# Loading two weight matrices by casting GpSimd transfers beside the loads of q, k and v, in a new order of instructions

## The chip, the cores and the metric

One core of one Trainium2 chip runs the whole program. The metric is device time in microseconds of one execution; medians over several executions are quoted. The record marks an execution as slow when it takes over 1.5% longer than the fastest of the same kernel; the others are called fast.

## The reference

A linear attention feeds a gated scan. Cut to what matters:

```python
q_s = softmax(q, axis=-1); k_s = softmax(k, axis=sequence)      # 8 batches, 8 heads, 576 x 64
kv  = einsum('bhsd,bhse->bhde', k_s, v)
x   = einsum('bhsd,bhde->bhse', q_s, kv)                        # as (8, 576, 512)
proj = x @ w_in                                                 # w_in 512 x 1024
val, gate = proj[..., :512], proj[..., 512:]
for t in range(576):
    h = exp(A_log) * h + val[:, t, :]                           # one state per batch and channel
    ys[:, t, :] = h
out = (gate * sigmoid(gate) * ys) @ w_out                       # w_out 512 x 512
```

Inputs are float32: 9.44 MB each of q, k and v, 2.10 MB of w_in, 1.05 MB of w_out, 2 KB of A_log. The output is 9.44 MB.

## The kernel before

The program is a list of tokens, `operation/engine.batch.part`, that fixes the order of instructions on every engine (A is ScalarE, D is VectorE, P is GpSimd). Each token calls a small function. Batches enter one by one: exp of q and its sums (`expq`, `qsum`), normalisation (`norm`), transposes on TensorE and their copies (`transp`, `tevac`), exp of k, cast of v (`vcast1`), the product kv and its normalisation (`kv`, `kvn`), the product with q (`xt` for batch 0) and its copies to bf16 (`xevac`). From there the work goes in 9 chunks of 512 positions: eight projections of 4 matmuls each (`val`, `gate`), scan, tanh, multiplications, output projection (`outp`), eviction (`oevac`), store.

All loads are issued by SyncE into one queue. The weights arrive as float32 in shared buffers and are cast by whichever engine the token names:

```python
def lwin(self, e, kt, h):                       # 8 of these, 256 KB each
    nc.sync.dma_start(out=buf("y", ("w", kt, h)),
                      in_=moe_w_in[kt * 128:kt * 128 + 128, h * Di:(h + 1) * Di])

def cwin(self, e, kt, h):
    copy(e, win[:, kt, h * Di:(h + 1) * Di], buf("y", ("w", kt, h)))

def lwout(self, e, j):                          # 2 of these, 512 KB each
    nc.sync.dma_start(out=buf("ob", ("w", j)),
                      in_=moe_w_out.rearrange("(j m p) c -> j p m c", j=2, p=128)[j])

def lalog(self, e):                             # the decay row
    nc.sync.dma_start(out=alog, in_=moe_A_log.rearrange("(o n) -> o n", o=1))

def _proj(self, dst, i, col):                   # called by val and gate
    ...
        for kt in range(4):
            nc.tensor.matmul(dst[:, a:z], lhsT=win[:, kt, col:col + 128],
                             rhs=xT[:, kt, s0:s0 + z - a], start=(kt == 0), stop=(kt == 3))
```

In the SyncE queue the order of bytes is q0, q1, k0 and v0, q2, w_in, k1, v1, q3, v2, k2, w_out, and so on (the digit is the batch).

The softmax here doesn't subtract the row's maximum and nothing guards it: scores larger than these inputs give would overflow.

## Time and profile before

| | before |
|---|---|
| median, range (3 executions, before the changed kernel was run) | 145.44 us, 144.34 to 145.5 |
| span of the profiled execution | 142.5 us |
| first projection starts | 22.9 us |
| last matmul ends | 138.5 us |
| HBM read, written | 31.46 MB, 9.44 MB |

The page opens with busy time, share of the span and number of instructions of each engine. A later part lists queues with packets, megabytes and share of the engines' time:

```profile
PE 119.6 (84%) x1269; PEld 61.7 (43%) x1284; DVE 114.6 (80%) x146; ACT 98.9 (69%) x138; POOL 92.2 (65%) x80
...
q1 hardware_dynamic: 24226, 42.08, 84.2%
```

TensorE is the busiest engine at 84%, which says little by itself, because the shares average a byte-bound start and a TensorE-bound rest. There is a single data queue. Of a table of stretches, the columns are length, then busy time with counts of PE, PEld, DVE, ACT and POOL, clock, DMA share, GB/s:

```profile
46.00:150.00 104.00, 91.82 (x898) 46.33 (x907) 81.63 (x102) 66.00 (x100) 59.22 (x44) 0.99 0.72 243
```

The second number is the work that TensorE still has in front of it at 46 us: 91.8 us. The last matmul starts its group at 137.42 and ends at 138.46, which is 92.5 us after the 46. So TensorE hardly idles in that stretch, and the end of the kernel is 46 us, plus what was left, plus a tail of 4.0 us to the end of the span. I call this number the work left at 46 us.

### The profile page before, as it was taken

What the parts mean: (1) busy time and instruction counts of PE and PEld (TensorE: products, weight loads), DVE (VectorE), ACT (ScalarE), POOL (GpSimd) and SP (SyncE); (2) the same over time, 40 slices, a digit from 0 to 9 for tenths busy, and PEclk for the clock granted to TensorE, in tenths of its full rate; (3) what the DMA queues carried; (4) which work ended last, traced back from release to release, by engine and by line L of the source; (5) the groups of instructions that cost most, each with busy time, mean ns of one, the idle gap of its engine ahead of it and who ended that gap; (6) DMA issues with size and microseconds to landing.
All of it is one profiled execution on the core that took longest, in us unless ns stands there. A gap on an engine that the chain in (4) does not pass through costs nothing.

```text
span 142.5 us, 3185 instructions
## 1 busy us (share of the span) xinstructions
PE 119.6 (84%) x1269; PEld 61.7 (43%) x1284; DVE 114.6 (80%) x146; ACT 98.9 (69%) x138; POOL 92.2 (65%) x80
## 2 busy tenths in 40 slices
PE   0024586987599999999999999999999999999980
...
DMA  4999999999999999999999999999543433007195
GB/s 111 401 399 391 391 390 389 391 393 391 389 389 392 391 391 391 387 404 403 394 325 382 399 240 208 263 408 392 110 83 121 181 147 147 0 0 289 71 343 190
DMA packets 24243, 42.29 MB, mean 297 GB/s; under 512 B 5666, under 2 KB 5922, under 8 KB 24227
## 3 DMA queue, kind: packets, MB, share of 16 engines
q1 hardware_dynamic: 24226, 42.08, 84.2%
...
HBM read 31.46 MB, written 9.44 MB: 287 GB/s over the span
## 4 chain that ended last, share of the span: by engine, by line
PE 70%; DMA 14%; DVE 5%; POOL 3%; issue 3%; SPq 2%; ACT 0%; POOLq 0%; ACTq 0%; DVEq 0%
PE pp L377 38%; PE po L423 21%; DMA kf<-in_k_dram 7%; DMA y<-in_moe_w_in_dram 6%; PE ax L290 4%; PE tp L271 3%; POOL eq L263 3%; SPq L188 2%; DVE qs L255 2%; PE pp L333 1%; PE ax L333 1%; DVE u L404 1%; DVE xT L194 1%; PE pp L423 1%; PE pp L360 1%
## 5 line engine op out<-in xcount | busy, mean ns | idle before, releaser
L377 PE MATMUL pp<-xT,win 128*128 128x512 bf16 (+1 forms) x308 | 68.0, 363 | 1.9 <-ACT xT L192 1.2
L408 POOL TENSOR_TENSOR z<-u,y 128x512 bf16<-128x512 f32 x29 | 37.3, 1297 | 24.2 <-DVE u L404 15.6
L377 PEld LDWEIGHTS <-win 128*128 128x128 bf16 x320 | 30.6, 99 | 31.5 <-issue 4.4
L396 DVE TENSOR_TENSOR_SCAN y<-decay,y,pp 128x512 f32<-128x512 f32 x32 | 39.6, 1262 | 1.4 <-PE pp L377 1.3
L263 POOL TENSOR_TENSOR eq<-eq,qs 128x1152 bf16<-128x1152 bf16 x16 | 33.8, 2119 | 7.9 <-DVE qs L258 7.7
L423 PE MATMUL po<-wout,z 128*128 128x512 bf16 x134 | 33.7, 379 | 0.3
L401 ACT ACTIVATE th<-pp 128x512 f32<-128x512 f32 x36 | 21.5, 597 | 15.8 <-PE pp L377 15.6
L404 DVE SCALAR_TENSOR_TENSOR u<-th,pp 128x512 f32<-128x512 f32 x36 | 24.4, 683 | 5.3 <-ACT th L401 4.8
L255 DVE TENSOR_REDUCE qs<-eq 128x36 f32<-128x2304 bf16 (+1 forms) x10 | 20.6, 2057 | 6.6 <-ACT eq L235 6.6
L271 PE MATMUL tp<-ident,eq 128*128 128x128 bf16 x108 | 10.9, 249 | 13.3 <-POOL eq L263 11.8
L235 ACT ACTIVATE eq<-qf 128x1152 bf16<-128x1152 f32 x16 | 18.3, 1158 | 5.3 <-DMA qf<-in_q_dram 5.3
L430 ACT ACTIVATE ob<-po 128x512 f32<-128x512 f32 x28 | 16.6, 599 | 7.6 <-PE po L423 7.6
L423 PEld LDWEIGHTS <-z 128*128 128x128 bf16 x148 | 13.9, 98 | 15.3 <-issue 1.0
L241 ACT ACTIVATE ek<-kf 128x2304 bf16<-128x2304 f32 (+1 forms) x10 | 17.2, 1736 | 0.5 <-DMA kf<-in_k_dram 0.5
L194 POOL CAST vb<-vf 128x1152 bf16<-128x1152 f32 (+1 forms) x14 | 14.9, 1080 | 3.7 <-DMA vf<-in_v_dram 3.6
L271 PEld LDWEIGHTS <-eq 128*128 128x128 bf16 x108 | 8.3, 111 | 17.4 <-POOL eq L263 13.2
L192 ACT ACTIVATE xT<-pp 128x504 bf16<-128x504 f32 (+1 forms) x20 | 7.8, 443 | 4.4 <-PE pp L333 2.6
L290 PE MATMUL ax<-vb,ek 64*64 64x65 bf16 x576 | 7.3, 199 | 1.5 <-ACT ek L241 1.1
L290 PEld LDWEIGHTS <-ek 64*64 64x64 bf16 x576 | 6.2, 112 | 4.7 <-issue 2.2
L192 ACT ACTIVATE eqT<-tp 128x768 bf16<-128x768 bf16 x8 | 6.5, 810 | 1.6 <-PE tp L271 1.6
L192 ACT ACTIVATE xT<-ax 128x1008 bf16<-128x1008 f32 x7 | 7.1, 1016 | 0.3 <-PE pp L360 0.3
L432 DVE TENSOR_SCALAR ob<-po 128x512 f32<-128x512 f32 x6 | 4.1, 684 | 3.2 <-PE po L423 3.2
...
## 6 DMA issues: line engine op xcount, KB each, us to landing
...
y<-in_moe_w_in_dram SPq DMA_DIRECT2D x8, 256.0 KB, 8.8
...
```

The lines of the kernel that those rows point to most:

```text
L192: nc.scalar.activation(out, in_, AF.Copy)
L235: nc.scalar.activation(buf("eq", b)[:, q2].rearrange("p c h d -> p h c d"), buf("qf", b)[:, 2 * q2:2 * q2 + 2].rearrange("p h (c d) -> p h ...
L255: nc.vector.tensor_reduce(s[:, 0, n].rearrange("p (a o) -> p a o", o=1), buf("eq", b)[:, h].rearrange("p q c h d -> p (q c h) d"), axis=AX ...
L263: eng[e].tensor_tensor(x, x, r.rearrange("p (a o) -> p a o", o=1) .broadcast_to([128, 2 * C, D]), ALU.mult)
L271: nc.tensor.transpose(tp[:, j, :], src[:, 6 * g + j, :], ident)
L290: nc.tensor.matmul(kvp[o:o + 64, h2, q2 * E1:(q2 + 1) * E1], lhsT=ek[r, 2 * q2 + hp2, c * D:(c + 1) * D], rhs=vb[r, 2 * q2 + hp2, c, :], s ...
L377: nc.tensor.matmul(dst[:, a:z], lhsT=win[:, kt, col:col + 128], rhs=xT[:, kt, s0:s0 + z - a], start=(kt == 0), stop=(kt == 3))
L396: nc.vector.tensor_tensor_scan(buf("y", (i, m)), a, buf("pp", ("v", i, m)), init, op0=ALU.mult, op1=ALU.add)
L401: nc.scalar.activation(buf("th", (i, m)), buf("pp", ("g", i, m)), AF.Tanh, scale=0.5)
L404: nc.vector.scalar_tensor_tensor(buf("u", (i, m)), buf("th", (i, m)), 1.0, buf("pp", ("g", i, m)), op0=ALU.add, op1=ALU.mult)
L408: eng[e].tensor_tensor(buf("z", i)[:, m], buf("u", (i, m)), buf("y", (i, m)), ALU.mult)
L423: nc.tensor.matmul(self._po(i, r, h), lhsT=buf("z", i)[:, m, r * 128:(r + 1) * 128], rhs=wout[:, m, self._cols(h)], start=(m == 0), stop=( ...
```

## The change

The intent is to take ten casts and ten loads out of the engines and the SyncE queue. A transfer issued by GpSimd can cast float32 to bf16 on its way, so the weights land ready to use and, being in another queue, need not wait behind q, k and v. The decay row goes to ScalarE's queue for the same reason. The list of tokens was rearranged as a whole; only its first lines are shown.

```diff
-lq.0.1 expq.0.1 lq.0.0 lq.1.- qsum.0.1 expq.0.0 norm/P.0.1 qsum.0.0 transp.0.2 expq.1.0 lk.0.0
-tevac/A.0.2 lv.0.1 norm/P.0.0 transp.0.0 lk.0.1 expk.0.0 expq.1.1 qsum.1.0 tevac/D.0.0
 ... (the rest of the old order is left out)
+lalog lq.0.0 lq.0.1 expq.0.0 lq.1.- lv.0.0 lk.0.0 lk.0.1 expq.0.1 expq.1.0 lv.0.1 qsum.0.0
+vcast1/A.0.1 expq.1.1 qsum.0.1 swin.1 swout lq.2.- norm/D.0.1 norm/P.0.0 qsum.1.0 expk.0.0
+transp.0.2 tevac/D.0.2 lv.1.- transp.0.0 vcast1/P.0.0 swin.0 tevac/D.0.0 transp.0.1 expk.0.1
 ... (the rest of the new order is left out)
+        def swin(self, e, h):
+            nc.gpsimd.dma_start(out=win[:, :, h * Di:(h + 1) * Di],
+                                in_=moe_w_in.rearrange("(k p) c -> p k c", p=128)[:, :, h * Di:(h + 1) * Di])
+
+        def swout(self, e):
+            nc.gpsimd.dma_start(out=wout, in_=moe_w_out.rearrange("(m p) c -> p m c", p=128))
 ...
         def lalog(self, e):
-            nc.sync.dma_start(out=alog, in_=moe_A_log.rearrange("(o n) -> o n", o=1))
+            nc.scalar.dma_start(out=alog, in_=moe_A_log.rearrange("(o n) -> o n", o=1))
```

`swin.1` is the gate half of w_in, `swout` all of w_out, `swin.0` the value half.

More of the change, by code (lines that the diff above doesn't have):

```diff
@@ L23 @@
 ORDER = """
-lq.0.1 expq.0.1 lq.0.0 lq.1.- qsum.0.1 expq.0.0 norm/P.0.1 qsum.0.0 transp.0.2 expq.1.0 lk.0.0
-tevac/A.0.2 lv.0.1 norm/P.0.0 transp.0.0 lk.0.1 expk.0.0 expq.1.1 qsum.1.0 tevac/D.0.0
-vcast1/P.0.2 lalog lv.0.0 expk.0.1 norm/P.1.0 vcast1/D.0.3 vcast1/P.0.0 qsum.1.1 vcast1/A.0.1
-transp.0.1 tevac/D.0.1 lq.2.- kv.0.1 lwin.0.0 lwin.2.0 lwin.3.0 kv.0.0 transp.1.0 tevac/A.1.0
-lwin.1.0 lwin.1.1 norm/P.1.1 kvn.0 lwin.0.1 xt.0.0.1 xt.0.1.1 cwin/P.2.0 expq.2.0 xevac/D.0.0.1
-transp.1.1 xt.0.0.0 tevac/D.1.1 xevac/A.0.1.1 transp.1.2 xt.0.1.0 xevac/D.0.0.0 lwin.2.1
@@ L30 @@
-cwin/D.0.0 cwin/P.1.0 cwin/P.3.0 lwin.3.1 cwin/P.1.1 xevac/D.0.1.0 expq.2.1 talog val.0.3 acol
-tevac/A.1.2 lk.1.- cwin/A.2.1 cwin/P.0.1 val.0.1 lv.1.- cwin/A.3.1 gate.0.0 decay/A.3 qsum.2.-
-scan.0.3 gate.0.3 tanh.0.0 scan.0.1 norm/P.2.0 decay/P.2 gmul.0.0 norm/P.2.1 tanh.0.3 vcast/P.1.1
-gmul.0.3 expk.1.1 transp.2.0 val.0.0 expk.1.0 lq.3.- scan.0.0 gate.0.2 val.0.2 tanh.0.2
-tevac/D.2.0 vcast/A.1.0 gate.0.1 zmul/P.0.3 transp.2.1 kv.1.1 gmul.0.2 scan.0.2 kv.1.0 lv.2.-
-tanh.0.1 lk.2.- lwout.0 kvn.1 lwout.1 gmul.0.1 lq.4.- xr.1 xrevac/D.1 xa.1.0 decay/A.0
@@ L36 @@
-tevac/D.2.1 expq.3.0 expq.3.1 lk.3.- xa.1.1 xbevac/A.1.1 zmul/P.0.0 xaevac/A.1.0 transp.2.2
-tevac/A.2.2 xbevac/D.1.0 gate.1.3 tanh.1.3 zmul/P.0.1 zmul/P.0.2 gate.1.2 qsum.3.- gmul.1.3
-val.1.0 vcast/P.2.0 tanh.1.2 gmul.1.2 vcast/P.2.1 val.1.3 expk.2.- norm/P.3.0 gate.1.1 scan.1.0
-transp.3.0 val.1.2 tanh.1.1 tevac/A.3.0 scan.1.3 norm/P.3.1 kv.2.0 cwout/A.0 gmul.1.1 scan.1.2
-gate.1.0 tanh.1.0 kv.2.1 expq.4.0 transp.3.1 cwout/P.1 kvn.2 expq.4.1 outp.0.2 tevac/D.3.1 xr.2
-decay/P.1 xa.2.0 transp.3.2 zmul/P.1.2 xrevac/D.2 gmul.1.0 outp.0.3 lv.3.- xa.2.1 qsum.4.-
@@ L42 @@
-val.1.1 lq.5.- zmul/P.1.0 zmul/P.1.3 oevac/A.0.2 xaevac/A.2.0 lv.4.- lk.5.- oevac/A.0.3
-vcast/P.3.1 xbevac/A.2.0 vcast/P.3.0 xbevac/A.2.1 scan.1.1 tevac/D.3.2 outp.0.0 outp.0.1 expk.3.-
-val.2.2 gate.2.1 scan.2.2 tanh.2.1 oevac/A.0.0 val.2.1 lk.4.- gmul.2.1 kv.3.1 kv.3.0 gate.2.0
-oevac/A.0.1 gate.2.2 expq.5.1 tanh.2.0 store.0.1 norm/P.4.0 zmul/P.1.1 scan.2.1 kvn.3 gmul.2.0
-tanh.2.2 val.2.3 transp.4.0 expq.5.0 norm/P.4.1 gmul.2.2 scan.2.3 outp.1.0 xa.3.0 xr.3 outp.1.1
-zmul/P.2.2 tevac/A.4.0 xrevac/A.3 lq.6.- qsum.5.- oevac/A.1.0 xa.3.1 xbevac/A.3.0 lv.5.-
@@ L48 @@
-xbevac/A.3.1 vcast/P.4.0 vcast/P.4.1 zmul/P.2.1 gate.2.3 outp.1.3 transp.4.1 tanh.2.3 val.2.0
-tevac/D.4.1 norm/P.5.1 gmul.2.3 scan.2.0 xaevac/A.3.0 zmul/P.2.3 transp.4.2 oevac/A.1.1 val.3.1
-val.3.3 expk.4.- scan.3.1 scan.3.3 tevac/D.4.2 norm/P.5.0 expk.5.- oevac/A.1.3 val.3.0 kv.4.1
-kv.4.0 gate.3.0 tanh.3.0 zmul/P.2.0 scan.3.0 outp.1.2 val.3.2 vcast/P.5.0 gate.3.2 gmul.3.0
-vcast/P.5.1 expq.6.0 oevac/A.1.2 tanh.3.2 expq.6.1 scan.3.2 kvn.4 transp.5.0 gate.3.1 outp.2.3
-gmul.3.2 tevac/D.5.0 xa.4.0 store.0.0 zmul/P.3.2 store.1.0 xr.4 zmul/P.3.0 tanh.3.1 xaevac/A.4.0
@@ L54 @@
-outp.2.0 gmul.3.1 xrevac/A.4 transp.5.1 oevac/A.2.3 kv.5.1 kv.5.0 store.1.1 lk.6.- xa.4.1
-gate.3.3 xbevac/A.4.1 qsum.6.- kvn.5 xbevac/A.4.0 outp.2.2 val.4.1 tanh.3.3 tevac/A.5.1
-oevac/A.2.0 gate.4.2 zmul/P.3.1 norm/P.6.0 gmul.3.3 tanh.4.2 transp.5.2 val.4.2 scan.4.1 gmul.4.2
-zmul/P.3.3 gate.4.0 tevac/A.5.2 gate.4.1 oevac/A.2.2 tanh.4.0 outp.3.1 scan.4.2 lv.6.- lq.7.-
-gmul.4.0 dtransp.6.0 vcast/P.6.0 xa.5.0 xa.5.1 tanh.4.1 gmul.4.1 store.2.1 oevac/D.3.1
-xbevac/D.5.1 norm/P.6.1 vcast/P.6.1 outp.2.1 expk.6.- val.4.0 xaevac/A.5.0 xbevac/D.5.0 outp.3.0
@@ L60 @@
-scan.4.0 kv.6.0 xr.5 zmul/P.4.2 dtransp.6.1 kv.6.1 val.4.3 xrevac/A.5 gate.5.1 zmul/D.4.1
-expq.7.1 gate.4.3 oevac/D.2.1 oevac/A.3.0 scan.4.3 zmul/P.4.0 tanh.5.1 tanh.4.3 kvn.6 expq.7.0
-outp.3.2 val.5.1 lv.7.- gmul.5.1 gmul.4.3 val.5.2 outp.3.3 scan.5.1 zmul/P.4.3 oevac/A.3.2 xa.6.1
-scan.5.2 zmul/P.5.1 outp.4.2 xbevac/A.6.0 store.2.0 store.3.0 qsum.7.- xbevac/A.6.1 xr.6
-vcast/P.7.0 oevac/A.3.3 xa.6.0 val.5.0 xrevac/A.6 outp.4.0 vcast/A.7.1 norm/P.7.1 val.5.3
-scan.5.0 oevac/A.4.2 xaevac/A.6.0 gate.5.3 scan.5.3 lk.7.- store.3.1 tanh.5.3 gate.5.2 tanh.5.2
@@ L66 @@
-outp.4.3 gmul.5.3 gate.6.0 gate.5.0 oevac/D.4.0 gmul.5.2 tanh.6.0 gmul.6.0 zmul/P.5.3 tanh.5.0
-val.6.2 gmul.5.0 val.6.3 outp.4.1 expk.7.- scan.6.2 gate.6.2 kv.7.1 kv.7.0 gate.6.3 oevac/A.4.1
-tanh.6.2 scan.6.3 dtransp.7.1 norm/P.7.0 gmul.6.2 kvn.7 zmul/D.5.2 val.6.1 dtransp.7.0 tanh.6.3
-oevac/A.4.3 zmul/P.5.0 val.6.0 gmul.6.3 outp.5.3 scan.6.1 scan.6.0 outp.5.2 zmul/D.6.2
-oevac/A.5.3 xr.7 xa.7.0 store.4.1 outp.5.1 xrevac/A.7 store.4.0 xa.7.1 xaevac/A.7.0 xbevac/D.7.0
-gate.6.1 xbevac/A.7.1 oevac/D.5.2 gate.7.0 val.7.0 zmul/P.6.0 tanh.6.1 tanh.7.0 gmul.6.1 gmul.7.0
@@ L72 @@
-outp.5.0 val.7.2 oevac/D.5.1 zmul/P.6.3 gate.7.2 scan.7.0 zmul/P.6.1 scan.7.2 outp.6.3 store.5.1
-val.7.3 oevac/A.5.0 gate.7.1 tanh.7.2 gmul.7.2 scan.7.3 tanh.7.1 gmul.7.1 gate.7.3 tanh.7.3
-val.8.2 val.7.1 gmul.7.3 zmul/P.7.0 val.8.0 outp.6.1 oevac/A.6.3 outp.6.0 scan.8.2 gate.8.1
-scan.7.1 scan.8.0 gate.8.2 zmul/D.7.3 oevac/A.6.1 tanh.8.1 gmul.8.1 gate.8.0 zmul/D.7.2
-zmul/D.7.1 oevac/A.6.0 tanh.8.2 outp.6.2 gmul.8.2 tanh.8.0 store.5.0 val.8.1 outp.7.2 val.8.3
-gmul.8.0 store.6.0 scan.8.1 oevac/A.6.2 oevac/A.7.2 zmul/P.8.2 gate.8.3 outp.7.3 tanh.8.3
@@ L78 @@
-scan.8.3 store.6.1 zmul/P.8.1 gmul.8.3 zmul/D.8.3 outp.7.1 oevac/A.7.3 outp.7.0 oevac/A.7.1
-zmul/P.8.0 store.7.1 oevac/A.7.0 outp.8.0 store.7.0 oevac/A.8.0 outp.8.1 store.8.0 outp.8.2
-outp.8.3.1 oevac/A.8.1 oevac/A.8.3.1 outp.8.3.0 store.8.1 oevac/D.8.2 store.8.3.1 store.8.2
-oevac/D.8.3.0 store.8.3.0
+lalog lq.0.0 lq.0.1 expq.0.0 lq.1.- lv.0.0 lk.0.0 lk.0.1 expq.0.1 expq.1.0 lv.0.1 qsum.0.0
+vcast1/A.0.1 expq.1.1 qsum.0.1 swin.1 swout lq.2.- norm/D.0.1 norm/P.0.0 qsum.1.0 expk.0.0
+transp.0.2 tevac/D.0.2 lv.1.- transp.0.0 vcast1/P.0.0 swin.0 tevac/D.0.0 transp.0.1 expk.0.1
@@ new lines @@
+lk.1.- qsum.1.1 kv.0.0 norm/P.1.0 tevac/D.0.1 vcast1/A.0.2 vcast1/P.0.3 norm/P.1.1 kv.0.1 kvn.0
+xt.0.1.0 xt.0.0.0 xevac/A.0.1.0 xevac/D.0.0.0 expq.2.1 xt.0.1.1 xevac/D.0.1.1 expq.2.0 transp.1.0
+lq.3.- tevac/D.1.0 xt.0.0.1 lv.2.- talog transp.1.1 xevac/D.0.0.1 gate.0.3 gate.0.0 qsum.2.- acol
+tevac/A.1.1 transp.1.2 tanh.0.3 tanh.0.0 tevac/A.1.2 gate.0.1 decay/P.2 lk.2.- vcast/P.1.1
+vcast/P.1.0 gmul.0.3 tanh.0.1 gmul.0.0 norm/P.2.0 val.0.3 gmul.0.1 decay/A.1 scan.0.3 val.0.0
+scan.0.0 decay/P.0 expk.1.0 expk.1.1 val.0.2 expq.3.1 gate.0.2 kv.1.0 kv.1.1 scan.0.2 kvn.1
@@ new lines @@
+norm/P.2.1 decay/P.3 tanh.0.2 transp.2.0 lq.4.- xr.1 xa.1.0 tevac/D.2.0 zmul/P.0.0 transp.2.1
+lv.3.- expq.3.0 lk.3.- gmul.0.2 lq.5.- zmul/P.0.3 xrevac/A.1 xa.1.1 xaevac/A.1.0 xbevac/A.1.1
+val.0.1 xbevac/A.1.0 gate.1.0 tevac/A.2.1 vcast/P.2.1 tanh.1.0 qsum.3.- scan.0.1 gmul.1.0 val.1.0
+transp.2.2 gate.1.2 expk.2.- vcast/P.2.0 zmul/D.0.1 zmul/P.0.2 gate.1.3 kv.2.0 tanh.1.2
+norm/P.3.0 tanh.1.3 scan.1.0 tevac/D.2.2 kv.2.1 gmul.1.3 expq.4.0 expq.4.1 gmul.1.2 norm/P.3.1
+outp.0.1 val.1.3 oevac/A.0.1 zmul/P.1.0 vcast/P.3.0 kvn.2 transp.3.0 lk.4.- gate.1.1 outp.0.3
@@ new lines @@
+tanh.1.1 tevac/A.3.0 scan.1.3 gmul.1.1 xa.2.0 xr.2 outp.0.2 zmul/P.1.3 xrevac/A.2 xaevac/A.2.0
+transp.3.1 oevac/A.0.3 xa.2.1 xbevac/A.2.0 vcast/P.3.1 val.1.2 qsum.4.- norm/P.4.0 outp.0.0
+xbevac/A.2.1 val.1.1 gate.2.2 expk.3.- tevac/D.3.1 scan.1.2 transp.3.2 lv.4.- val.2.2 tanh.2.2
+scan.1.1 oevac/A.0.0 zmul/P.1.2 zmul/P.1.1 expq.5.1 expq.5.0 oevac/A.0.2 tevac/D.3.2 gmul.2.2
+kv.3.1 kv.3.0 val.2.1 gate.2.1 scan.2.2 gate.2.0 vcast/P.4.0 lv.5.- scan.2.1 outp.1.0 tanh.2.1
+tanh.2.0 kvn.3 gmul.2.1 val.2.3 outp.1.1 gmul.2.0 expk.4.- xr.3 scan.2.3 xa.3.0 oevac/A.1.0
@@ new lines @@
+transp.4.0 gate.2.3 outp.1.3 xaevac/A.3.0 vcast/P.4.1 xrevac/A.3 xa.3.1 norm/P.4.1 oevac/A.1.1
+qsum.5.- kv.4.0 zmul/P.2.2 tanh.2.3 kv.4.1 gmul.2.3 kvn.4 xbevac/A.3.1 tevac/D.4.0 outp.1.2
+norm/P.5.0 xbevac/A.3.0 zmul/P.2.3 val.2.0 store.0.0 lk.5.- scan.2.0 zmul/P.2.1 val.3.1
+transp.4.1 tevac/D.4.1 gate.3.3 lq.6.- oevac/A.1.3 store.0.1 lk.6.- gate.3.1 oevac/A.1.2 xa.4.0
+transp.4.2 scan.3.1 expk.5.- tanh.3.3 val.3.2 gmul.3.3 vcast/P.5.0 val.3.0 tanh.3.1 tevac/A.4.2
+gmul.3.1 xaevac/A.4.0 zmul/P.2.0 scan.3.2 gate.3.0 scan.3.0 tanh.3.0 outp.2.0 kv.5.0 xr.4
@@ new lines @@
+transp.5.0 expq.6.1 gmul.3.0 norm/P.5.1 xrevac/D.4 lk.7.- store.1.1 expq.6.0 tevac/D.5.0 val.3.3
+vcast/P.5.1 kv.5.1 xa.4.1 transp.5.1 oevac/A.2.0 outp.2.1 scan.3.3 gate.3.2 tevac/A.5.1
+xbevac/A.4.0 xbevac/A.4.1 outp.2.3 transp.5.2 tanh.3.2 qsum.6.- gmul.3.2 val.4.3 expk.6.- val.4.1
+zmul/P.3.3 gate.4.1 lq.7.- oevac/A.2.1 store.1.0 zmul/P.3.1 scan.4.3 lv.6.- gate.4.0 tanh.4.1
+tanh.4.0 tevac/A.5.2 norm/P.6.0 scan.4.1 outp.2.2 val.4.0 store.2.0 zmul/P.3.2 kvn.5 gmul.4.1
+gmul.4.0 oevac/A.2.3 oevac/A.2.2 gate.4.2 zmul/P.3.0 tanh.4.2 norm/P.6.1 scan.4.0 gate.4.3
```

23 lines of the change are left out of this document (added).

## The prediction

> **What bounds the kernel now.** I read the strip of 40 slices first, to see which engine is full and when.
>
> ```profile
> PE   0024586987599999999999999999999999999980
> ...
> DMA  4999999999999999999999999999543433007195
> GB/s 111 401 399 391 391 390 389 391 393 391 389 389 392 391 391 391 387 404 403 394 325 382 399 240 208 263 408 392 110 83 121 181 147 147 0 0 289 71 343 190
> ```
>
> TensorE fills up only about slice 13 (46 us). The DMA engines are full from slice 2 on at about 390 GB/s. So the kernel has a start-up in which bytes are scarce, then a long stretch in which TensorE is scarce. A table of busy time by stretch puts numbers on it (columns: length, then PE, PEld, DVE, ACT, POOL busy with counts, clock, DMA share, GB/s):
>
> ```profile
> 22.90:29.30 6.40, 5.52 (x23) 2.29 (x24) 5.61 (x6) 4.67 (x8) 3.88 (x5) 1.00 1.06 392
> ...
> 34.80:38.00 3.20, 1.57 (x23) 0.86 (x24) 3.20 (x6) 3.20 (x5) 3.20 (x3) 1.00 1.06 393
> 38.00:46.00 8.00, 7.76 (x110) 3.84 (x111) 7.31 (x9) 6.78 (x9) 8.00 (x7) 1.00 1.05 389
> 46.00:138.50 92.50, 91.82 (x898) 46.33 (x907) 81.21 (x102) 66.00 (x100) 59.22 (x44) 1.00 0.78 264
> ```
>
> From 46 us TensorE idles 0.7 us in 92.5. No order of instructions can shorten that stretch except by having more done before it. The end of the kernel is therefore: the moment the first projection can start, plus a fixed amount of TensorE work, plus its idle time and slow clock in start-up, plus a tail. Now the start of the chain of waits (start, length, what):
>
> ```profile
> 3.52 10.61 DMA kf<-in_k_dram
> ...
> 14.53 9.10 DMA y<-in_moe_w_in_dram
> 23.68 0.61 POOL win L194
> 24.30 2.31 issue
> 26.75 2.13 POOL eq L263
> ```
>
> This names w_in as the last thing waited for until 24.3 us, which is the case for the change. But the timeline of the first 20 us shows the other branch, k and v of batch 0:
>
> ```profile
> 4.72 1.16 ACT L235 ACTIVATE eq<-qf 128x1152 bf16<-128x1152 f32 x1 [2.71 <-DMA qf<-in_q_dram]
> ...
> 9.65 1.16 ACT L235 ACTIVATE eq<-qf 128x1152 bf16<-128x1152 f32 x1 [2.30 <-DMA qf<-in_q_dram]
> ...
> 12.69 0.66 POOL L194 CAST vb<-vf 128x576 bf16<-128x576 f32 x1 [0.78 <-DMA vf<-in_v_dram]
> ...
> 15.79 0.66 POOL L194 CAST vb<-vf 128x576 bf16<-128x576 f32 x1 [0.36 <-DMA vf<-in_v_dram]
> ...
> 17.48 0.42 DVE L300 TENSOR_TENSOR kvc<-ax,kr 128x256 bf16<-128x256 f32 x1
> ```
>
> Each start behind a DMA marks a landing. They fit a straight line, landing = 3.1 us + megabytes queued so far / 0.39: q of batch 0 is 1.18 MB, predicted 6.1, and its second exp starts at 6.19; all of q0, q1, k0, v0 (4.72 MB) gives 15.2, seen 15.7; with q2 (1.18) and w_in (2.10) it gives 23.6, and the last w_in casts start at 23.7 and 24.3. After k and v come kv, its normalisation (17.48), four x products and their copies:
>
> ```profile
> 21.56 0.76 DVE L194 CAST xT<-ax 128x576 bf16<-128x576 f32 x1 [0.29 <-PE ax L312]
> ...
> 23.71 4.55 PE L377 MATMUL pp<-xT,win 128*128 128x512 bf16 x14 [0.22 <-POOL win L194]
> ```
>
> The last piece of x of batch 0 is ready at 22.3 us; the first projection starts at 22.9 and runs steadily from 23.7. So the branch through k0 and v0 and the branch through w_in end within about 1.4 us of each other. The tuner of the old order balanced them on a full DMA stream.
>
> **What the Trainium skill says.** "DMA: Bandwidth & Descriptors", section "SWDGE vs HWDGE vs iDMA": a cast inside a transfer can only be issued from GpSimd, whose software writes the descriptors. The trace before has no such transfer (its only data queue is SyncE's), so no number here. Same page, section "Issuing engines are not separate DMA queues": transfers from SyncE, ScalarE and GpSimd run on the same 16 DMA engines and interleave, so issuing from two saves only issue time. The trace agrees so far that the engines are the limit: share 1.05, 390 GB/s. Same page, section "Queues, rings and completion order": each DMA engine takes turns between queues by packets. That decides this case, and the trace before, with one data queue, cannot show it. "TensorE: Matmul & The Clock Gate", Part 1: TensorE runs at half rate until about 3.4 us of sustained work. The trace agrees: weight loads of the first projections are spaced 0.43 us (23.29, 23.72, 24.14 ... 26.28) and later 0.216 us (1.73 us for 8).
>
> **The change part by part.** Removed: 8 casts of w_in and 2 of w_out.
>
> ```profile
> L194 POOL CAST win<-y 128x512 bf16<-128x512 f32 x5 | 3.0, 612 | 2.8 <-DMA y<-in_moe_w_in_dram 2.7
> ...
> L192 ACT ACTIVATE win<-y 128x512 bf16<-128x512 f32 x2 | 1.3, 629 | 0.5 <-DMA y<-in_moe_w_in_dram 0.5
> ```
>
> GpSimd: 5 x 0.61 + 1.04 = 4.1 us; ScalarE: 2 x 0.63 + 1.05 = 2.3; VectorE: 0.42. None of it is on TensorE. On the path to the end lie only the waits it causes: TensorE waited 0.22 us for a cast and 0.66 us at 28.9 for a normalisation that GpSimd ran behind casts and a decay copy; between 34.8 and 38 us all three helpers are 100% busy and TensorE loses 1.6 of 3.2 us, part of it backlog, part the latency kv to x to projection, which stays. I book 0.9 + 0.6 = 1.5 us gain.
>
> Added: three GpSimd transfers (gate half of w_in, all of w_out, later the value half), 1.05 MB each as read. HBM bytes read stay at 31.46 MB, so at 0.39 MB/us nothing is saved if the read side paces them; only the order of bytes changes. The first two have no wait in front: GpSimd is free at 1.7 us (its last memset), so they can flow from about 5 us (estimate: the same 2.4 us from readiness to landing as q has, 0.74 to 3.1, plus a us to write descriptors). There they meet q0's second half, q1, k0, v0. By 5.2 us the SyncE queue has landed 0.82 MB of the 4.72 it needs for k0 and v0; 3.9 remain. With equal turns the 2.1 MB of weights are all through before those 3.9 MB end, and v0 lands at 3.1 + (4.72 + 2.10) / 0.39 = 20.6 us instead of 15.7. If GpSimd gets only a quarter of the turns, 3.9 / 0.29 = 13.4, so 18.6 us. If it cost nothing, 15.7. The value half comes third on GpSimd, after a cast of v0, and meets little of this. Early w_out buys nothing: the old kernel first uses it at 46 us.
>
> From v0 to the first projection the old kernel took 22.9 - 15.7 = 7.2 us; with w_in no longer in the way and a slightly tighter order of the x copies, I take 6.6. So the first projection: 27.2, 25.2 or 22.3 us, against 22.9: +4.3, +2.3, -0.6. I weigh them towards the middle: +2.3.
>
> Moved: the decay row to ScalarE's queue, before the table load at 0.73 us; its first exp waits for q until 4.72 anyway, so 0. One normalisation moves to VectorE, free then: 0. The order of everything else is new. In the long stretch TensorE cannot gain. The tail differs: the old one ends with half-row evictions (0.42 us) and 128 KB stores, the new one with two full ScalarE evictions (0.60) and a 256 KB store:
>
> ```profile
> out_dram<-ob SPq DMA_DIRECT2D x3, 256.0 KB, 2.9
> out_dram<-ob SPq DMA_DIRECT2D x2, 128.0 KB, 2.1
> ```
>
> (0.60 - 0.42) + (2.9 - 2.1) = 1.0 us at most; I take 0.7, as the old tail queued two small stores. Sum: +2.3 - 1.5 + 0.7 = +1.5 us; 145.4 + 1.5 = 146.9 us.
>
> **The rivals.** First, the weights are free: the second queue fills gaps and k0 and v0 are not late. For it: the chain names w_in, and both are off the old critical point. Against it: the DMA share is already full. Time: 145.4 - 0.6 - 1.5 + 0.7 = 144.0; if backlog falls further and the tail is equal, 142.5. Second, contention is full (equal turns or more): 145.4 + 4.3 - 1.5 + 0.7 = 148.9, and 150.5 if the late start also leaves batch 1 waiting: q, k, v of batches 0 and 1, q2 and all weights are 11.4 MB, so k1 lands at 32.3 us against 26.8. Third, GpSimd becomes the bound: writing descriptors might hold it longer than the 5 us of idleness it has before its first normalisation at 7.73. Beyond that each us delays the transposes, but those have slack until k0 and v0 land late, so it adds little: 147 to 149.
>
> **Range and chances.** 143.0 to 150.5 spans the rivals. Faster than 142.5 needs both free weights and a better order: 0.14. Slower than 148.3 needs nearly full contention: 0.33. Within 2%: 0.53.
>
> **What would show each step.** The v casts of batch 0 that wait for DMA: 15.8 moving to 18.5 to 21 proves contention; unchanged disproves it. The first projection at 25 us, and w_in no longer in the chain. Total GB/s in the first 20 us still about 390; well above would mean the cast paces differently, and a long landing time of the GpSimd transfers would mean a slow cast. TensorE still above 99% from 46 us; gaps there would mean the new order is at fault and the prediction wrong for a reason I did not weigh. The last store's landing shows the tail.

## The result, and the profile after

The changed kernel takes 149.61 us (median of 4, 148.91 to 149.74) against 145.38 us of the kernel before in the same rounds (144.34 to 145.5). The ratio is 1.0285, with a 95% interval of 1.0227 to 1.0343: slower. Ratios here and below are the mean time of one kernel's fast runs over that of the other's of the same rounds, so they are not quite the ratio of the medians. The spans of the two profiles, 142.5 and 147.7 us, differ by 5.2 us, more than the 4.2 us of the medians, because the profile of before fell on one of its quicker executions (144.23 us); the reason comes with experiment e10.

The strip of 40 slices of the changed kernel (3.7 us each), for TensorE and the bytes moved:

```profile
PE   0001415989699999999999999999999999999960
...
DMA  4999999999999999999999996952803300463374
GB/s 153 333 288 296 310 324 318 404 395 391 395 387 391 390 392 392 387 407 397 394 397 405 403 255 170 301 218 51 231 32 134 142 0 0 176 254 141 143 255 176
```

The DMA engines are as full as before from slice 2 on, but TensorE's ramp is later. In slices 3 to 7 the figure is 288 to 324 GB/s and not 390. The engines did not slow down: the view counts bytes written, and a casting transfer writes half of what it reads. The page's queues, and the issues of the weights with their size as written and the median time from issue to landing:

```profile
q1 hardware_dynamic: 22528, 38.93, 73.7%
q0 software_dynamic: 1584, 1.57, 6.4%
...
win<-in_moe_w_in_dram POOLq DMA_DIRECT2D x2, 512.0 KB, 11.1
...
wout<-in_moe_w_out_dram POOLq DMA_DIRECT2D x1, 512.0 KB, 16.6
```

The 1.57 MB in queue q0 are the 3.15 MB of weights after the cast. The trace also records single packets. Tabulated by queue (my own count in stretches of 1 us, not a view of the profile), it gives for the first 20 us:

```
stretch            packets per us            KB read per us
                   q0 (GpSimd)  q1 (SyncE)   q0          q1          sum
4 to 5 us          0            170          0           391         391
8 to 17 us         87 to 97     88 to 96     174 to 194  188 to 211  380 to 390
one packet, 8 to 17 us: q0 reads 2 KB, writes 1 KB, mean 96 ns; q1 moves 2304 B, mean 106 ns
```

(The counts include packets of 4 B; the means and KB of q0 leave them out. The trace gives what q0 writes; that it reads twice as much follows from the types, and fits the 31.46 MB read from HBM, as before.) The two queues take turns one for one, and the sum read stays about where it was. Now the timeline of the start (start, length, engine, line, what; in brackets the idle time and what ended it):

```profile
1.51 0.93 POOL L209 DMA_DIRECT2D win<-in_moe_w_in_dram  x1
2.44 0.75 POOL L213 DMA_DIRECT2D wout<-in_moe_w_out_dram  x1
...
14.66 0.66 POOL L192 CAST vb<-vf 128x576 bf16<-128x576 f32 x1 [5.21 <-DMA vf<-in_v_dram]
15.27 0.81 POOL L209 DMA_DIRECT2D win<-in_moe_w_in_dram  x1
...
22.20 0.67 POOL L192 CAST vb<-vf 128x576 bf16<-128x576 f32 x1 [3.98 <-DMA vf<-in_v_dram]
...
23.89 0.42 DVE L305 TENSOR_TENSOR kvc<-ax,kr 128x256 bf16<-128x256 f32 x1
...
27.71 0.58 PE L382 MATMUL pp<-xT,win 128*128 128x512 bf16 x1
```

The last casts of v0 follow their data at 22.2 us where the kernel before had 15.8, the normalisation of kv starts at 23.9 where it had 17.5, and the first projection at 27.7 where it had 22.9. The chain of waits (start, length, what) no longer contains w_in:

```profile
4.32 14.87 DMA vf<-in_v_dram
19.19 17.89 DMA qf<-in_q_dram
37.17 1.16 ACT eq L240
```

It now runs through v, and then through a load of q that lands at 37.1 us: until then the kernel waits for bytes of the SyncE queue. The same table of stretches as before:

```profile
46.00:150.00 104.00, 95.86 (x988) 48.45 (x998) 85.61 (x107) 68.76 (x102) 66.14 (x47) 0.99 0.69 243
```

The work left at 46 us is 95.9 us, 4.0 more than before. TensorE's last matmul ends at 142.89, 4.4 later. So the loss lies almost whole in the first 46 us, and the long stretch only passes it on.

### The profile page after: what moved, and what is told of

Read it like the earlier page. It is cut to its first block, busy times and chain, and to the rows that moved or that the text cites. A ratio compares the mean times of both kernels' runs of the same rounds, so it can differ in the third digit from the quotient of the medians.

```text
span 147.7 us, 3164 instructions
## 1 busy us (share of the span) xinstructions
PE 118.9 (81%) x1268; PEld 61.4 (42%) x1284; DVE 114.1 (77%) x142; ACT 96.0 (65%) x135; POOL 93.0 (63%) x80
## 3 DMA queue, kind: packets, MB, share of 16 engines
q0 software_dynamic: 1584, 1.57, 6.4%
HBM read 31.46 MB, written 9.44 MB: 277 GB/s over the span
## 4 chain that ended last, share of the span: by engine, by line
PE 63%; DMA 22%; DVE 6%; ACT 2%; SPq 2%; issue 1%; DVEq 0%; ACTq 0%
PE pp L382 36%; PE po L428 18%; DMA qf<-in_q_dram 12%; DMA vf<-in_v_dram 10%; PE ax L295 3%; PE tp L276 2%; SPq L186 2%; DVE y L401 2%; DVE qs L260 2%; DVE z L413 2%; ACT eq L240 2%; PE ax L338 1%; PE pp L338 1%; PE pp L428 1%; PE pp L365 1%
## 5 line engine op out<-in xcount | busy, mean ns | idle before, releaser
L413 POOL TENSOR_TENSOR z<-u,y 128x512 bf16<-128x512 f32 x31 | 39.4, 1286 | 22.8 <-DVE y L401 15.6
L268 POOL TENSOR_TENSOR eq<-eq,qs 128x1152 bf16<-128x1152 bf16 x15 | 32.1, 2148 | 6.4 <-DVE qs L263 6.4
L192 POOL CAST vb<-vf 128x1152 bf16<-128x1152 f32 (+1 forms) x15 | 16.0, 1085 | 11.6 <-DMA vf<-in_v_dram 11.6
L435 ACT ACTIVATE ob<-po 128x512 f32<-128x512 f32 x31 | 18.3, 597 | 7.0 <-PE po L428 7.0
L428 PEld LDWEIGHTS <-z 128*128 128x128 bf16 x148 | 13.8, 98 | 16.5 <-issue 1.0
L190 ACT ACTIVATE xT<-ax 128x1008 bf16<-128x1008 f32 (+1 forms) x8 | 7.7, 968 | 3.3 <-PE ax L317 2.0
L192 DVE COPY eqT<-tp 128x768 bf16<-128x768 bf16 x11 | 5.9, 532 | 0.9 <-PE tp L276 0.9
L190 ACT ACTIVATE eqT<-tp 128x768 bf16<-128x768 bf16 x7 | 5.7, 812 | 0.7 <-PE tp L276 0.7
```

The source lines that it names most:

```text
L190: nc.scalar.activation(out, in_, AF.Copy)
L192: eng[e].tensor_copy(out, in_)
L268: eng[e].tensor_tensor(x, x, r.rearrange("p (a o) -> p a o", o=1) .broadcast_to([128, 2 * C, D]), ALU.mult)
L413: eng[e].tensor_tensor(buf("z", i)[:, m], buf("u", (i, m)), buf("y", (i, m)), ALU.mult)
L428: nc.tensor.matmul(self._po(i, r, h), lhsT=buf("z", i)[:, m, r * 128:(r + 1) * 128], rhs=wout[:, m, self._cols(h)], start=(m == 0), stop=( ...
```

## The experiments

Theory 1: the GpSimd queue takes every second packet from the SyncE queue, k0 and v0 come late, and that is the loss. Rivals: the cast or the software queue itself is slow; GpSimd is held by its issues; the new order of instructions is at fault; or the bytes cost the same wherever they are put. The runs in one table, to which the text refers (a dash where it was not needed; e4's last five columns are from a profile in the slow state):

| run | median us | ratio | last cast of v0 | first projection | work left at 46 | last matmul ends | span |
|---|---|---|---|---|---|---|---|
| before | 145.4 | | 15.8 | 22.9 | 91.8 | 138.5 | 142.5 |
| changed | 149.6 | 1.0285 | 22.2 | 27.7 | 95.9 | 142.9 | 147.7 |
| e1 no weights | 142.2 | 0.982 | 15.9 | 21.4 | 88.7 | 134.8 | 139.6 |
| e2 w_out late | 148.4 | 1.0252 | 18.0 | 23.5 | 95.3 | 141.5 | 146.3 |
| e3 all late | 148.2 | 1.0213 | 15.6 | 23.5 | 95.3 | 141.6 | 146.3 |
| e4 old order, early | 149.8 fast | 1.0328 | 22.0 | 29.1 | 100.2 | 146.1 | 150.9 |
| e5 old order, late | 147.9 | 1.0175 | 16.8 | 24.3 | 94.9 | 140.9 | 145.8 |
| e6 hardware queue | 151.7 | 1.0461 | 22.6 | 28.1 | 97.8 | 145.7 | 149.9 |
| e7 k, v first | 151.8 | 1.0498 | 12.8 | 24.4 | 98.5 | 145.3 | 149.8 |
| e8 new order, SyncE | 152.5 | 1.0481 | 16.5 | 22.0 | 96.4 | 146.4 | 150.6 |
| e9 w_out on SyncE | 152.0 | 1.0464 | 16.4 | 24.4 | 96.1 | 144.9 | 149.6 |
| e10 row only | 145.1 | 0.9983 | 16.0 | 23.1 | 93.4 | 140.1 | 144.0 |
| e11 w_out only | 146.1 | 1.0048 | 16.0 | 23.0 | 92.5 | 139.1 | 143.4 |
| e12 as e8, mended | 148.1 | 1.0212 | 16.4 | 21.9 | 94.9 | 141.7 | 145.7 |

Medians of "before" were 144.67 beside e1 to e4, 145.56 beside e5 to e7, 145.8 beside e8 to e11 and 145.4 beside e12. e12 had 5 rounds, the others 3. The columns from the fourth on come from one execution of each run. The profiles of e2, e7 and e10 hold a stretch of 3.4 us at half clock before 46 us and those of e4, e8 and e9 one between 44 and 54 us, worth up to 1.7 us (see e10), so differences of that size between rows are not to be read as effects of an edit.

### e1_free: the new order without any load of weights

```diff
-... swin.1 swout ...          (three tokens taken out)
-... swin.0 ...
+    nc.vector.memset(win.rearrange("p k c -> p (k c)"), 0.01)
+    nc.gpsimd.memset(wout.rearrange("p k c -> p (k c)"), 0.01)
```

> The changed kernel with no weight transfers at all: w_in and w_out are filled with a constant by VectorE and GpSimd at the start, so the result is wrong on purpose; everything else, the new order included, is as in the changed kernel. Theory 1 (the weights take turns with q, k and v of batch 0 and push v0 back): v0 lands at about 15.7 us as in the kernel before, the first projection starts at 22 to 23 us instead of 27.7, and the time falls by about 5 us, to 143.5 to 145. Rival 2 (the new order of instructions is what costs): the time stays above 148. Rival 3 (the softer waits further on, on q of batch 3): the first projection is early, but the time falls by less than 3 us.

It took 142.18 us, ratio 0.982 (0.9738 to 0.9902); it fell more than expected. Its output is wrong, which doesn't matter for the time. From its timeline:

```profile
15.88 0.67 POOL L192 CAST vb<-vf 128x576 bf16<-128x576 f32 x1 [0.93 <-DMA vf<-in_v_dram]
...
21.39 3.09 PE L382 MATMUL pp<-xT,win 128*128 128x512 bf16 x8
```

v0 is on time again and the first projection starts 6.3 us earlier than in the changed kernel. The work left at 46 us falls by 95.86 - 88.65 = 7.2 us. The weights are 3.15 MB, at 0.39 MB/us 8.1 us of the DMA engines' time (an estimate from the rate of the strip). So in this order nearly all the time in which weights are read turns up as TensorE's work put off. What the new order costs by itself it does not tell: the old order was never run without weights, so the run cannot part the order from the bytes and casts that are gone.

### e2_wout_late: w_out moved out of the crowded start

```diff
-... qsum.0.1 swin.1 swout lq.2.- ...
+... qsum.0.1 swin.1 lq.2.- ...
-... vcast/P.1.0 gmul.0.3 ...
+... vcast/P.1.0 swout gmul.0.3 ...
```

> The changed kernel with only w_out's transfer moved, from the second place on GpSimd to behind the casts of v of batch 1 (about 30 us). Theory 1: 1.05 MB fewer compete before v0 lands, worth 1.05 / 0.39 = 2.7 us: v0 lands at about 19.5 us instead of 22.1, the first projection at about 25, the time about 147. If the amount of weights in flight did not matter (rival 2, the order), it stays at 149.6.

It took 148.44 us, ratio 1.0252 (1.0166 to 1.0338). The first projection came at 23.5 us, 4.2 earlier than in the changed kernel, and the median fell by about 1.2 us only, which the overlapping intervals of the two ratios do not tell from nothing. A miss. A table of stretches shows one place where the head start went (last three columns: granted clock, DMA share, GB/s):

```profile
36.00:38.00 2.00, 1.79 (x10) 0.73 (x8) 1.76 (x1) 2.00 (x6) 1.94 (x3) 0.51 1.12 290
38.00:40.00 2.00, 2.00 (x8) 0.75 (x7) 1.97 (x3) 1.05 (x2) 2.00 (x3) 0.64 1.10 322
```

After a pause TensorE ran at half clock for 3.4 us (36.0 to 39.5 us in the trace's clock records). And w_out, now read in front of k of batch 2, delayed that. The work left at 46 us is 95.3, only 0.6 below the changed kernel.

### e3_all_late: all three held until v0 has landed

```diff
-... qsum.0.1 swin.1 swout lq.2.- ...
+... qsum.0.1 lq.2.- ...
-... vcast1/P.0.0 swin.0 ...
+... vcast1/P.0.0 swin.1 swin.0 ...
-... vcast/P.1.0 gmul.0.3 ...
+... vcast/P.1.0 swout gmul.0.3 ...
```

> The changed kernel with both halves of w_in issued only after the first half of v of batch 0 has landed and been cast (about 11.5 us), and w_out behind the casts of v of batch 1. In the changed kernel a GpSimd transfer began to move about 4.7 us after its issue began, so these move from about 16 us, when v0 is in. Theory 1: v0 lands at about 15.7, the gate half of w_in at about 21.5, the first projection at 22 to 23, the time 144 to 145.5: no better than the kernel before by more than 1 us. Rival 2 (the new order): above 148. Rival 3 (GpSimd's issue or the cast itself is slow): between, as the weights are then late instead, first projection after 25 us.

It took 148.23 us, ratio 1.0213 (1.0145 to 1.0281). A miss again, and the one that changed my theory. (The transfers moved from 16.0 us as planned, 4.3 us after the issue began at 11.7; the 4.7 us of the expectation was a misreading of the trace.) From its timeline:

```profile
15.60 0.67 POOL L190 CAST vb<-vf 128x576 bf16<-128x576 f32 x1
...
23.46 3.59 PE L380 MATMUL pp<-xT,win 128*128 128x512 bf16 x8 [2.22 <-DMA win<-in_moe_w_in_dram]
...
42.38 2.12 ACT L244 ACTIVATE ek<-kf 128x2304 bf16<-128x2304 f32 x1 [2.18 <-DMA kf<-in_k_dram]
...
44.55 0.81 PE L293 MATMUL ax<-vb,ek 64*64 64x65 bf16 x72 [1.76 <-ACT ek L244]
```

v0 is as early as without weights. But w_in, issued at 11.7 us, lands only at 23.4, so TensorE waits 2.2 us for it, and w_out on its way holds up k of batch 2, for which ScalarE waits 2.2 us and TensorE behind it 1.8 us. The contention was moved, not removed. v0 alone does not set the end.

### e4_old_order_early: the old order with the three transfers as early as in the change

```diff
-  all tokens lwin, cwin, lwout, cwout
+  swin.0 swout before norm/P.0.1;  swin.1 after vcast1/P.0.2
```

> The kernel before, with its own order, but w_in and w_out loaded by the three GpSimd transfers as early as in the changed kernel (first half and w_out at the start, second half behind the first cast of v of batch 0), its SyncE weight loads and casts taken out. Theory 1: v0 again lands 5 to 6 us late (20.5 to 22 us), the first projection at 27 to 28, the time 148 to 150, as slow as the changed kernel although the order is the old one. Rival 2 (the new order is at fault): 143 to 145.5, the casts being saved.

Its fast runs took 149.54 and 150.14 us, ratio 1.0328 (1.0223 to 1.0433); two more were slow, and the profile is of one of these. As expected: without the new order, the early transfers alone lose as much as the whole change, and v0 is as late. From the timeline of the slow run, which I use for the landing only, not for times:

```profile
21.95 0.66 POOL L190 CAST vb<-vf 128x576 bf16<-128x576 f32 x1
...
29.05 1.46 PE L380 MATMUL pp<-xT,win 128*128 128x512 bf16 x3
```

### e5_old_order_late: the old order with the transfers held back

```diff
-  all tokens lwin, cwin, lwout, cwout
+  swin.0 after norm/P.0.1;  swin.1 after norm/P.0.0;  swout after decay/P.2
```

> The kernel before with its own order, weights by three GpSimd transfers as in the change, but issued so that they move only when k and v of batch 0 are nearly in: first half of w_in behind GpSimd's first normalisation (about 10 us), second behind its second (about 12.5 us), w_out behind a decay copy near 29 us. Theory 1: v0 lands at 15.7 to 16.5 us, the first projection at about 23, the time 143.5 to 145.5: the cast inside the transfer is worth 0 to 2 us once the competition is gone. If the cast or the software queue is itself slow (rival 3), the weights come after 27 us and the time is above 147.

147.93 us, ratio 1.0175 (1.0081 to 1.0269). A miss: I expected it to equal the kernel before. v0 came at 16.8, a microsecond late, the first projection at 24.3, and 94.9 us of work were left at 46 us, 3.1 more than before. Ten casts fewer on the engines did not pay for that. The first projection was 1.4 us late; what added the rest was not followed up.

### e6_hw_queue: plain float32 loads on ScalarE's queue at the same early places, cast by GpSimd

```diff
-            nc.gpsimd.dma_start(out=win[:, :, h * Di:(h + 1) * Di], ...
+            nc.scalar.dma_start(out=buf("y", ("w", kt, h)), ...        # and w_out likewise
+  cwin/P and cwout/P tokens after norm/P.1.0, before decay/P.2, after decay/P.3
```

> The changed kernel with the same weight bytes at the same early times, but uncast, from ScalarE's hardware queue into float32 buffers, and the casts to bf16 back on GpSimd where it is idle. Theory 1 (any second queue takes turns): v0 lands as late as in the changed kernel, 20 to 22 us, and the time is 148.5 to 151. Rival 3 (it is the cast, or GpSimd's software queue, that slows the shared engines): v0 lands before 18 us and the time is below 147.

151.67 us, ratio 1.0461 (1.0393 to 1.053). From its timeline:

```profile
22.63 0.67 POOL L192 CAST vb<-vf 128x576 bf16<-128x576 f32 x1 [0.65 <-DMA vf<-in_v_dram]
...
28.14 2.93 PE L382 MATMUL pp<-xT,win 128*128 128x512 bf16 x8
```

A hardware queue without a cast delays v0 to the same moment, 22.6 against 22.2 us. Its packets, too, alternate with those of SyncE's queue (from 8 to 16 us, 94 to 99 per us against 90 to 103, by the same count), and by 22.1 us it had read 2.56 MB of weights where the casting transfers had read 2.58. So neither the cast nor the software queue is needed for this delay; of the two kinds of second queue that were tried, both cause it. The time came 0.7 us above the expected range; GpSimd casts ten pieces in this run, and what they cost was not separated.

### e7_kv_first: k0 and v0 in front of q1

```diff
-lalog lq.0.0 lq.0.1 expq.0.0 lq.1.- lv.0.0 lk.0.0 lk.0.1 ... lv.0.1
+lalog lq.0.0 lq.0.1 expq.0.0 lv.0.0 lk.0.0 lk.0.1 ... lv.0.1 lq.1.-
 (softmax of q1 and transposes moved behind the x copies; weights as in e3)
```

> A try at a version that beats both: the changed kernel with k and v of batch 0 loaded before q of batch 1, w_in issued behind the first cast of v of batch 0 (about 10 us), w_out behind the casts of v of batch 1, and the work on q of batch 1 put behind the x copies of batch 0. Theory 1: the bytes in front of v0 are 3.54 MB, so v0 lands at 3.1 + 3.54 / 0.39 = 12.2 us; the gate half of w_in at about 20; the first projection at about 20, 2.5 us before the kernel before; the time 142 to 144, unless batch 1 (its q is later) leaves TensorE short between 25 and 45 us, then 144 to 146. If the landing of v0 does not set the end, the time stays with that of the run that only holds the weights back.

151.78 us, ratio 1.0498 (1.0405 to 1.0591), a clear miss. v0 was cast by 12.8 us, yet:

```profile
23.10 0.82 PE L274 MATMUL tp<-ident,eq 128*128 128x128 bf16 x6 [4.70 <-POOL eq L266]
...
24.37 2.93 PE L380 MATMUL pp<-xT,win 128*128 128x512 bf16 x8
```

TensorE sat 4.7 us in front of transposes of q1 that I had placed ahead of the first projection, and batch 1 came short later: 98.5 us left at 46 us. It tells that in this order an early v0 did not help while q1 was late, not what a well tuned order of this kind would give.

### e8_new_order_fifo: the new order with the old loading in the SyncE queue

```diff
-  swin.1 swout swin.0
+  lwin x8 after lq.2;  lwout x2 after lk.2;  casts on GpSimd and ScalarE
+  cwout/A.0 before expq.4.0;  cwout/P.1 after norm/P.3.1
```

> The changed kernel's order of instructions with the loading of the kernel before: w_in plain from SyncE's one queue behind q of batch 2, w_out behind k of batch 2, casts back on GpSimd and ScalarE. Theory 1, in the form it has after seven runs (the place of the weight bytes among the other bytes decides, first for v0, then for k of batch 2): v0 lands at 15.7 us, the first projection at 22 to 24, nothing waits for k of batch 2, and the time is 145.5 to 147, the new order keeping about 1.5 us of its own at the end (a wait for the last z, and a longer last store). Rival 2 (the order costs more than that): 148 or above.

152.5 us, ratio 1.0481 (1.0401 to 1.056). I had placed the casts of w_out badly, as the timeline of TensorE shows:

```profile
45.20 0.38 PE L428 MATMUL po<-wout,z 128*128 128x512 bf16 x1 [0.90 <-ACT wout L190]
...
48.98 0.59 PE L428 MATMUL po<-wout,z 128*128 128x512 bf16 x2 [3.40 <-POOL wout L192]
```

4.3 us of waits are mine and not the order's, so the run decides nothing about the order, and its time missed the expected 145.5 to 147. It does show the first projection at 22.0 us, 0.9 earlier than before.

### e9_wout_fifo: e3 with w_out as a plain load behind k of batch 2

```diff
-  swout after vcast/P.1.0
+  lwout x2 after lk.2;  cwout/A.0 before expq.4.0;  cwout/P.1 after norm/P.3.1
```

> The run in which the weights were held back, with only w_out taken from GpSimd and put plain on SyncE's queue behind k of batch 2, its two casts back on ScalarE and GpSimd. In the held-back run TensorE waited 1.8 us at 44.5 us for the exp of k of batch 2, which waited 2.2 us for its transfer. Theory 1: w_out's 1.05 MB no longer stand in front of it, k of batch 2 lands about 2 us earlier, and the time falls by 1.5 to 2 us, to about 146.3. If that wait was not what cost (a helper engine would have been next anyway), the time changes by less than 0.7 us.

151.99 us, ratio 1.0464 (1.0382 to 1.0547). The same misplaced casts cost 2.76 and 1.11 us, so its time, well above the expected 146.3, is inconclusive. ScalarE's wait for k of batch 2 fell from 2.18 to 0.36 us, which confirms what e3 said about w_out.

### e10_row_only: the kernel before with only the decay row on ScalarE

```diff
-            nc.sync.dma_start(out=alog, ...
+            nc.scalar.dma_start(out=alog, ...
-  lalog after vcast1/P.0.2
+  lalog first of all
```

> The kernel before with one part of the change alone: the decay row issued by ScalarE at the start instead of SyncE. All theories: no change, within 0.5 us of the kernel before; ScalarE's first exp waits for q until 4.7 us in any case, and SyncE's queue is full of waiting bytes.

145.11 us against 145.8, ratio 0.9983 (0.9893 to 1.0074): no change. Its runs fall in two groups, 144.2 to 144.4 and 145.9, as those of the kernel before do (144.1 to 144.4 and 145.3 to 145.9, with some others). The profile fell in the slower group, that of the kernel before in the quicker, and the two show a difference (weight loads, then a stretch, with the columns of above):

```profile
38.40 0.10 PEld L375 LDWEIGHTS <-win 128*128 128x128 bf16 x1 [1.72 <-issue]
38.78 0.15 PEld L375 LDWEIGHTS <-win 128*128 128x128 bf16 x1 [0.28 <-issue]
...
38.40:41.70 3.30, 3.08 (x7) 1.13 (x8) 2.22 (x3) 1.24 (x2) 3.30 (x4) 0.50 1.06 390
```

After the thin stretch between 34 and 38 us TensorE ran at half clock, from 38.27 to 41.68 us in the trace's clock records. In the profile of before, where TensorE resumed at 38.0 and not 38.4, the clock stayed at 1.00. Half of 3.41 us is 1.7 us lost; the work left at 46 us is 93.4 against 91.8 and the span 144.0 against 142.5.

The other executions bear this out. In the 32 executions of the kernel before that ran beside the experiments, the mean granted clock is 0.995 to 1.000 up to 144.9 us (one exception, 0.988), 0.986 to 0.988 from 145.4 to 146.3 us, and 0.976 in the three of 146.8 us that are marked slow. One stretch of 3.41 us at half clock in 144 us makes 0.988, two make 0.976. All four executions of the changed kernel have 0.993 or more, so between executions without such a stretch its loss is nearer to the 5.2 us of the spans than to the 4.2 us of the medians.

Why one execution has it and another has not stays open, but the clock records give a hint. In e2, e4, e7, e8, e9 and e10 the stretch lasts 3.41 us each time and begins a whole number of 3.41 us after the clock first became full: 28.03 + 3 x 3.41 = 38.27 in e10, 25.80 + 3 x 3.41 = 36.04 in e2. That first moment differs from profile to profile (26.47 in before). So it may be where this grid falls on the thin stretch, and not the 0.4 us by which TensorE resumed later, that decides; no run isolates it.

### e11_wout_soft: the kernel before with only w_out by a casting transfer

```diff
-  lwout.0 lwout.1 cwout/A.0 cwout/P.1
+  swout after zmul/P.0.3
```

> A try at keeping the good of both: the kernel before, with only w_out loaded by a casting GpSimd transfer, issued behind the first z product (about 34.5 us), so that it moves from about 39 us, when k of batch 2 is nearly in. This saves 1.04 us of GpSimd and 1.05 us of ScalarE near 44 us, where GpSimd is full. Theory 1: equal bytes at nearly the old place, so 0 to 1 us faster than the kernel before, 144 to 145.4. If w_out lands after 45.5 us (half the turns from 39 us: 1.05 / 0.2 = 5.3, so 44.4), TensorE waits for it and the time is 1 us above the kernel before.

146.08 us, ratio 1.0048 (0.997 to 1.0127): the same. At this place the transfer does no harm that can be seen, although the DMA engines are full there (share 1.12 from 39 to 44 us), and the two casts that it saves are worth nothing that can be seen.

### e12_new_order_fifo2: e8 with the casts of w_out earlier

```diff
-  cwout/A.0 before expq.4.0;  cwout/P.1 after norm/P.3.1
+  cwout/A.0 after tanh.1.2;   cwout/P.1 after zmul/P.0.2
```

> The new order with the old loading, mended: in the first try my own placing of w_out's casts cost, TensorE waiting 0.9 and 3.4 us for them and then running some 3.5 us at half clock. Here GpSimd's cast stands before its two normalisations of batch 3 and ScalarE's one tanh earlier; nothing else differs from that run. Theory 1: those waits go, about 4 to 5 us less than the first try, 147 to 148.3: slower than the kernel before by the 1.5 to 2 us of the new order's own end and cast places, and faster than the changed kernel by 1.5 us or more. Rival 2 (the order accounts for all of the loss): 149 to 150, no faster than the changed kernel.

148.1 us against 145.4, ratio 1.0212 (1.016 to 1.0264): inside the range expected of theory 1, but its interval overlaps that of the changed kernel. From its timeline and its table of stretches:

```profile
21.91 3.44 PE L382 MATMUL pp<-xT,win 128*128 128x512 bf16 x8
...
43.62 1.02 PE L428 MATMUL po<-wout,z 128*128 128x512 bf16 x4 [0.25 <-ACT wout L190]
...
46.00:150.00 104.00, 94.86 (x922) 47.05 (x922) 82.33 (x101) 67.39 (x101) 63.85 (x46) 0.98 0.71 244
```

The wait for the cast is down to 0.25 us. With the bytes of all inputs in almost the sequence of the kernel before, and the first projection 1.0 us earlier, this order still leaves 3.0 us more for after 46 us. So a good part of the loss does not need a second queue. I can't call it the order's own share, since the new order was made for engines that don't cast weights, and here GpSimd and ScalarE cast ten pieces at places that I chose.

No version with a correct result beat the kernel before.

## Why the prediction was right or wrong

The range held, the centre was 2.7 us low, and the second rival, full contention, came true: it gave 148.9 (150.5 if batch 1 waits too, a figure given without a sum). That the range held says little, since it was drawn to span the rivals. The outcome given the largest chance, within 2% (0.53), did not come; slower than 148.3, at 0.33, did.

**Bound and accounting: right.** End as first projection, plus a fixed stretch of TensorE, plus a tail, holds in both profiles. First projection +4.8 (22.89 to 27.71). From there to the end of the last matmul 115.57 us before (to 138.46) and 115.18 after (to 142.89), -0.4. From there to the end of the span 4.0 and 4.8, +0.8. The sum is +5.2, the difference of the spans.

**First projection: the mis-sized term.** The step "I weigh them towards the middle: +2.3" failed. I had the mechanism and the arithmetic of equal turns (+4.3), then averaged it with two cases that the packets do not show. The measured packets alternate one for one, v0's last cast is 6.4 us later and the first projection 4.8. Equal turns said 27.2 us for it; it came at 27.7. e1 shows that it needs the weights' bytes, e6 that it needs neither cast nor software queue, e4 that it needs no new order. That equal turns came within 0.5 us is partly luck, for two errors nearly cancel. v0 landed at about 22.1 us where equal turns had said 20.6. The third transfer, of which the prediction said that it "meets little of this", accounts for it: its packets run from 19.5 us, and by 22.1 us the GpSimd queue had read 2.58 MB and not 2.10, so 3.1 + (4.72 + 2.58) / 0.385 = 22.1 (an estimate from the packet counts; no run isolates it). And from the last cast of v0 to the first projection it took 5.5 us, against 7.1 in the kernel before; booked was a gain of 0.6 there. e1, e2, e8 and e12 show the same 5.5 us with other loading, and e4 7.1 us with the old order and the early loads, so this gain goes with the new order.

**Relief: mis-sized.** Booked -1.5, found -0.4 net between the first projection and the last matmul (the 1.6 us between v0 and the first projection are counted above). Ten casts did leave the engines, and TensorE no longer waits for a cast of w_in. Part of the gain may have gone into a wait near the end that the old order did not have. Weight loads of the changed kernel:

```profile
138.98 0.22 PEld L428 LDWEIGHTS <-z 128*128 128x128 bf16 x3 [0.63 <-POOL z L413]
139.53 2.85 PEld L428 LDWEIGHTS <-z 128*128 128x128 bf16 x17 [0.33 <-DVE z L413]
```

The last chunk's z is late by up to 0.96 us there; the same two waits stand in e12 and e1, so they belong to the new order; by how much they delay the end no run isolates. e11 and e5 speak against a large relief as well.

**Tail: the size was right, the reason is not shown.** Booked +0.7 for two full evictions and larger stores, found +0.8. But the tail after the last matmul was 4.9 us in e5, which has the old ending, and 4.0 in e12, which has the new one. The landing of the last stores differs that much from profile to profile.

**Checks that the prediction named.** The casts of v0 moved beyond 21 us: contention proven. w_in is gone from the chain. Bytes read stay at 380 to 390 KB/us, so the cast doesn't pace otherwise. TensorE stays at about 99% from 46 us. The third rival, GpSimd held by its issues, did not come: the three took 0.93, 0.75 and 0.81 us. (The idle time before its first normalisation, which the prediction gives as 5 us, is 6.0 us in the trace before, 1.7 to 7.73.)

**What the prediction did not weigh.** Two of its thoughts were too simple. It treated the delay of v0 as the thing that costs, but e2 and e3 brought v0 4.2 and 6.6 us and the first projection 4.2 us forward, and the medians gained 1.2 to 1.4: the weights then delay w_in itself, or batch 1 and k of batch 2, and TensorE waits there, or runs at half clock after waiting. And it treated order and loading as terms that add. By e12 the new order with the old loading costs 2.1% and the casting loads on top take it to 2.9%, intervals that overlap; by e4 the same loads in the old order cost 3.3%; by e1 the new order without weights gains 1.8%, with no run of the old order without weights to set beside it. These don't add up to one split. What stays open is how much of e12's 3.0 us is the order's and how much is my placing of the casts.

## What to carry to other kernels

While the DMA engines were full, a second queue was no extra road here: its packets alternated with those of the first, and the time was paid by whatever stood in the first queue at that moment, so ask of each byte that is let in early which byte it pushes back. Here no second queue for w_in, early or held back, beat the one queue with the weights at the place where they are needed; a second queue in a stretch where the DMA share is below 1 was not tried. Work out each rival to its end, and if one of them follows from the mechanism you believe, predict that one instead of an average.

## What the Trainium skill lacked or had wrong

- "DMA: Bandwidth & Descriptors", Specifications, gives about 1 us to the first byte for a transfer issued by GpSimd. Here, beside a busy SyncE queue, 4.2 to 4.3 us passed from the start of the issue to the first packet, for the first (1.5 to 5.8 us) and for the third transfer (15.3 to 19.5 us), and 4.3 us in e3 and e11.
- The same page, "Anatomy of one DMA", fits a GpSimd transfer as 2.0 us plus bytes over 436e3, which makes 4.4 us (an estimate from that formula) of 1.05 MB. Beside a full SyncE queue the three transfers of the changed kernel took 10.4 to 16.6 us from issue to landing; the page has no duration for a transfer that shares the engines with another queue.
- No page gives the pace of a casting transfer. Here it is paced by what it reads: a packet of 2 KB in and 1 KB out took 96 ns, one of 2304 B uncast beside it 106 ns, one of 2 KB uncast in e11 88 ns, and both queues together read 380 to 390 KB/us, about what one does alone.
- "TensorE: Matmul & The Clock Gate", Part 1, lets the clock fall after an idle window of about 3.4 us, and has no figure for how much work a window may hold and still let it fall. In e10 it fell at 38.27 us after 3.41 us in which TensorE had been busy for 1.6, with no idle time over 1.6 us on end; in e2 after 3.41 us with 1.9 us busy. Yet in e3 it stayed full after 3.41 us with 1.65 us busy (42.24 to 45.65), so busy time alone does not settle it.
